# Hash attention with a SwiGLU block: four hash products side by side in batch one, the late hash block moved behind the sums

## The chip, the cores and the metric

The kernel runs on one core of one Trainium2 chip. The metric is the time of one execution on the device in microseconds (us); less is better. All runs of this study were correct and in the fast state. Single executions of one kernel differ by up to 5 us (the kernel before: 1007.44 to 1012.0 in 30 runs of one session), most by 1 to 3, so differences near 1 us are judged by ratios over many runs and by the traces together. Each run's record also has the mean clock that the chip granted to TensorE, 1.000 being full. Short names: PE is TensorE's matmul stream, PEld its weight loads, DVE is VectorE, ACT ScalarE, POOL GpSimd, SP the engine whose queue issues most transfers.

## The reference, cut to what matters

Four batches of eight heads, 768 positions, head size 64. A query may see a key only where both fall into the same hash bucket. The attention output goes through a SwiGLU block.

```python
q_bits = (np.einsum('bhsd,dk->bhsk', q, proj) > 0)      # proj: 64 x 6
k_bits = (np.einsum('bhsd,dk->bhsk', k, proj) > 0)
mask = q_bucket[:, :, :, None] == k_bucket[:, :, None, :]   # buckets: the bits as one number
scores = np.where(mask, scale * q @ k.T, -1e9)
attn = softmax(scores)                                  # sum + 1e-9 below
out = attn @ v
# then, on x = out with the heads side by side (3072 x 512):
y = (silu(x @ w_gate) * (x @ w_val)) @ w_out            # 512 -> 1536 -> 512
```

## The kernel before

Heads are handled in pairs, four pairs to a batch. Scores are formed transposed. The mask is a second product added to them: each side has a bf16 tile (`kb`, `qb`) of signs, six per head, and k's signs are multiplied by a large constant, so that one differing bit pushes the score far below. The tile has rows 0 to 31 for scores of head 0 and rows 64 to 95 for head 1; a per-row factor clears the bits of the other head.

```python
def score(u):                       # six units (c = 0..5) a half, two halves a pair
    for x, start in ((T, True), (bits, False)):       # scores, then the mask
        for h in range(2):
            nc.tensor.matmul(sc[h], x["k", n][rows, ks], x["q", n][rows, qs], ...)
    for h in range(2):
        nc.scalar.activation(weights(u)[:, h, 0:HQ], sc[h], AF.Exp, scale=SCALE)

def sign(name, half, to, ps):
    o = bits[name, n][to, half * HQ : (half + 1) * HQ]          # HQ = 384
    nc.scalar.activation(o, ps, AF.Sign, bias=nudge[to])
    if name == "k":
        return lambda: nc.vector.tensor_scalar(o, o, scalar1=times_k[to], ..., op0=ALU.mult)

def hash_bits(name, half):          # first batch: one product of full width (128 columns)
    ps = bank("hps")
    nc.tensor.matmul(ps[:, 0:HQ], hash_w, T[name, n][:, half * HQ : (half + 1) * HQ], ...)
    return [sign(name, half, slice(0, P), ps[:, 0:HQ])]

def hash_blocks():                  # later pairs: four products of 32 columns in one bank
    tile_ = bank("hps")
    for i, (name, half) in enumerate(...):
        nc.tensor.matmul(tile_[i * 32 : (i + 1) * 32, 0:HQ], hash_w[:, 0:32], T[name, n][...], ...)
    # ... then two signs for each of them (rows 0 and rows 64), eight in all,
    # and four multiplies on VectorE for k

def total(n):                       # softmax sums of a pair, and their reciprocals
    # four 32-column products, VectorE's reciprocal, then eight transfers on SyncE's queue
    # that spread the reciprocals to the rows of the attention output; later norm(n)
    ...
```

The order of work for half a pair, from the main loop:

```python
for c in range(NCH):
    score(u + c)
    if c == 1 and half == 0 and 0 < n <= NP: total(n - 1)      # batch one and its successor
    if c: add(u + c)                                           # VectorE sums the weights
...
for c in range(NCH): attend(u + c)
...
if half == 1 and n >= NP: total(n)
# from batch two on: some 56 projection passes of an earlier batch (in "atoms") come here, and
# the "chores" of the next pair stand among them:
chores = [None, steps.pop(0), None, steps.pop(0)] if half == 0 else [None, steps.pop(0)]
```

So in the second half of each later pair the hash block stands after the first eight projection passes. Up projections are shown as `up`, down projections as `po`.

The softmax here doesn't subtract the row's maximum and nothing guards it: scores larger than these inputs give would overflow.

## Time and profile before

| kernel before | |
|---|---|
| time, 3 first runs | 1008.49 us median (1008.31 to 1009.91) |
| profiled execution | span 1005.4 us, granted clock 1.000 |
| TensorE busy | 999.8 us (99%) |
| VectorE, ScalarE, GpSimd busy | 574.7, 417.4, 98.7 us |

The prediction below shows the chain and VectorE's timeline. One view must be added, because it became important later: the busy time by stretches of 20 us. Columns are the stretch, its length, then for PE, PEld, DVE, ACT and POOL the busy us and instructions, then the granted TensorE clock (1.00 is full), the DMA share and GB/s.

```profile
40.00:60.00 20.00, 20.00 (x125) 9.29 (x123) 16.33 (x24) 15.64 (x37) 4.27 (x8) 1.00 0.71 212
100.00:120.00 20.00, 19.63 (x109) 8.81 (x109) 17.06 (x22) 11.31 (x25) 3.25 (x6) 1.00 0.62 191
```

PE is busy in nearly every us of batch one, and its clock is at 1.00 in all of it. VectorE is busy for 16 to 17 of 20 us by the records, although it stands waiting only once a pair; the rest is the small gaps between its instructions. A busy share therefore does not say which of the two sets the pace.

### The profile page before, as it was taken

What the parts mean: (1) busy time and instruction counts of PE and PEld (TensorE: products, weight loads), DVE (VectorE), ACT (ScalarE), POOL (GpSimd) and SP (SyncE); (2) the same over time, 40 slices, a digit from 0 to 9 for tenths busy, and PEclk for the clock granted to TensorE, in tenths of its full rate; (3) what the DMA queues carried; (4) which work ended last, traced back from release to release, by engine and by line L of the source; (5) the groups of instructions that cost most, each with busy time, mean ns of one, the idle gap of its engine ahead of it and who ended that gap; (6) DMA issues with size and microseconds to landing.
All of it is one profiled execution on the core that took longest, in us unless ns stands there. A gap on an engine that the chain in (4) does not pass through costs nothing.

```text
span 1005.4 us, 12486 instructions
## 1 busy us (share of the span) xinstructions
PE 999.8 (99%) x4597; PEld 603.9 (60%) x4597; DVE 574.7 (57%) x919; ACT 417.4 (42%) x921; POOL 98.7 (10%) x192
## 2 busy tenths in 40 slices
PE   9999999999999999999999999999999999999998
PEld 4444455555576775555557776555555787555687
DVE  4788898887883624556464543545557342435421
ACT  7777457575424215335351323435444201222200
POOL 2222132231000000000000000000000000111000
PEclk9999999999999999999999999999999999999999
DMA  7777495886213032433331304242122011323101
GB/s 229 200 257 228 145 243 156 229 279 169 76 39 78 22 95 67 101 97 92 95 105 28 72 17 115 76 102 84 54 85 78 22 37 63 105 76 113 32 27 37
DMA packets 120029, 106.21 MB, mean 106 GB/s; under 512 B 89024, under 2 KB 103360, under 8 KB 119968
## 3 DMA queue, kind: packets, MB, share of 16 engines
q0 software_dynamic: 19104, 73.28, 22.8%
q1 hardware_dynamic: 100064, 31.94, 14.0%
q8 instruction: 36, 0.59, 0.3%
q10 hardware_dynamic: 800, 0.20, 0.1%
q14 instruction: 25, 0.20, 0.1%
HBM read 81.79 MB, written 17.30 MB: 99 GB/s over the span
## 4 chain that ended last, share of the span: by engine, by line
PE 89%; DVE 7%; SPq 2%; issue 1%; DMA 1%; DVEq 0%; ACT 0%
PE up L544 42%; PE po L544 21%; PE sc L455 12%; PE av L469 10%; SPq L513 2%; DVE acc L487 1%; PE sum L500 1%; DVE wo L508 1%; PE hps L402 1%; DMA wo<-wo 1%; DVE room L294 1%; PE hps L394 1%; DVE room L326 0%; DVE room L349 0%; DVE xT L520 0%
## 5 line engine op out<-in xcount | busy, mean ns | idle before, releaser
L544 PE MATMUL up<-xT,room 128*128 128x384 f32 x768 | 263.7, 490 | 0.4 <-DVE xT L520 0.4
L544 PEld LDWEIGHTS up<-xT,room 128*128 128x128 f32 x768 | 144.2, 190 | 110.3 <-issue 15.4
L544 PE MATMUL up<-xc,room 128*128 128x384 f32 x576 | 197.4, 487 | 0.0
L455 PE MATMUL sc<-qT,kT 64*128 64x384 f32 x768 | 160.3, 494 | 0.0
L544 PEld LDWEIGHTS up<-xc,room 128*128 128x128 f32 x576 | 109.7, 191 | 76.0 <-ACT hid L607 0.2
L548 DVE TENSOR_TENSOR c<-c,up 128x384 f32<-128x384 f32 x72 | 39.8, 553 | 179.7 <-PE up L544 178.5
L487 DVE TENSOR_TENSOR acc<-acc,A 128x768 f32<-128x768 f32 x128 | 122.7, 958 | 15.4 <-ACT A L458 2.6
L308 POOL DMA_DIRECT2D room<-ram x96 | 51.9, 541 | 717.9 <-PE up L544 710.3
L458 ACT ACTIVATE A<-sc 128x384 f32<-128x384 f32 x256 | 105.4, 505 | 4.9 <-PE sc L455 4.7
L679 ACT COPY o<-po 128x256 f32<-128x256 f32 x48 | 17.9, 372 | 196.5 <-PE po L544 196.5
L455 PEld LDWEIGHTS sc<-qT,kT 64*128 64x128 f32 x768 | 68.0, 187 | 50.7 <-issue 43.3
L469 PE MATMUL av<-A,vraw 128*64 128x384 f32 (+1 forms) x512 | 88.2, 487 | 0.0
L530 ACT ACTIVATE th<-c 128x384 f32<-128x384 f32 x72 | 37.6, 523 | 110.9 <-DVE c L531 83.4
L548 DVE TENSOR_TENSOR o<-o,po 128x256 f32<-128x256 f32 x36 | 15.1, 421 | 111.6 <-PE po L544 82.4
L458 ACT ACTIVATE room<-sc 128x384 f32<-128x384 f32 x128 | 54.4, 495 | 33.6 <-PE sc L455 33.6
L544 PE MATMUL po<-wo,hid 128*128 128x256 f32 x288 | 66.9, 382 | 0.0
L544 PE MATMUL po<-wo,room 128*128 128x256 f32 x288 | 66.6, 381 | 0.2 <-DVE room L548 0.2
L544 PE MATMUL po<-room,hid 128*128 128x256 f32 x288 | 66.1, 380 | 0.0
L607 ACT COPY c<-up 128x384 f32<-128x384 f32 x72 | 34.4, 478 | 74.5 <-PE up L544 74.3
L455 PE MATMUL sc<-qb,kb 64*128 64x384 bf16 x384 | 65.2, 323 | 0.0
L469 PEld LDWEIGHTS av<-A,vraw 128*64 128x64 f32 x512 | 36.8, 137 | 46.0 <-issue 45.4
L544 PEld LDWEIGHTS po<-wo,hid 128*128 128x128 f32 x288 | 54.2, 190 | 12.0 <-issue 4.9
(109 smaller groups left out, 998.3 us busy)
## 6 DMA issues: line engine op xcount, KB each, us to landing
room<-ram POOLq DMA_DIRECT2D x48, 512.0 KB, 4.7
room<-ram POOLq DMA_DIRECT2D x48, 384.0 KB, 3.9
vraw<-in_v_dram SPq DMA_DIRECT2D x16, 384.0 KB, 3.3
ram<-room POOLq DMA_DIRECT2D x12, 512.0 KB, 4.7
out_dram<-o SPq DMA_DIRECT2D x48, 128.0 KB, 1.7
room<-in_moe_w_out_dram POOLq DMA_DIRECT2D x10, 512.0 KB, 6.7
qraw<-in_q_dram SPq DMA_DIRECT2D x48, 96.0 KB, 3.1
hid<-in_moe_w_gate_dram POOLq DMA_DIRECT2D x9, 512.0 KB, 6.2
```

What stands on the lines that cost most here:

```text
L294: nc.vector.scalar_tensor_tensor(out=wi, in0=hi, scalar=-(1 << 31), in1=wi, op0=ALU.bitwise_and, op1=ALU.bitwise_or)
L308: nc.gpsimd.dma_start(places[k % 2][:, PARTS[go], :], ram[k % NG][:, PARTS[go], :])
L455: nc.tensor.matmul(sc[h], x["k", n][rows, ks], x["q", n][rows, qs], start=start, stop=not start)
L458: nc.scalar.activation(weights(u)[:, h, 0:HQ], sc[h], AF.Exp, scale=SCALE)
L469: nc.tensor.matmul(ps[h * D : (h + 1) * D, 0:width], raws["v", n][:, h, c, :], a[:, h, 0:width], start=c == 0, stop=c == NCH - 1)
L487: nc.vector.tensor_tensor(acc[n, half], acc[n, half], a[:, :, 0:HQ], op=ALU.add)
L513: nc.sync.dma_start(t[at : at + BLOCK, half, :], r[g : g + BLOCK, :])
L530: nc.scalar.activation(th, g, AF.Tanh, scale=0.5)
L544: nc.tensor.matmul(ps, a, x, start=start and i == 0, stop=i == len(pairs_) - 1, skip_group_check=True)
L548: nc.vector.tensor_tensor(o, a, b, op=op)
L607: nc.scalar.copy(tile_of(g, spot), c)
L679: nc.scalar.copy(o, c)
```

## The change

The intent was to take work off TensorE and ScalarE. All hash products become 32 columns wide and stand side by side, in batch one too. Only the low rows get their signs from ScalarE, one 32x384 sign per product. The high rows are made from the low ones ("spread"): k's by a VectorE multiply, q's by a VectorE copy in batch one and by a transfer later. Late hash blocks stand directly behind the sums; in batch one the block of the next pair stands behind the last score unit of a pair. The transposes of the first pair's second half move into its first two score units. The core of the diff, with cuts marked:

```diff
-    hash_w = konst.tile([P, P], FP32, tag="hash", name="hash")
+    hash_w = konst.tile([P, BLOCK], FP32, tag="hash", name="hash")
 ...
+    for t in (sides["k", 0], sides["q", 0], sides["q", 1]):
+        nc.gpsimd.memset(t, 0.0)
 ...
-        def hash_bits(name, half): ...
-        def hash_blocks(): ...          # two signs each, four multiplies
+        def hash_blocks(todo, own):
             tile_ = bank("hps")
+            for i, (name, half) in enumerate(todo):
+                nc.tensor.matmul(tile_[i * BLOCK : (i + 1) * BLOCK, 0:HQ], hash_w, ...)
+            low, high = slice(0, BLOCK), slice(D, D + BLOCK)
+            def sign(i, name, half):
+                nc.scalar.activation(bits[name, n][low, half * HQ : (half + 1) * HQ],
+                                     tile_[i * BLOCK : (i + 1) * BLOCK, 0:HQ], AF.Sign, bias=nudge)
+            def spread():
+                for name in sorted({name for name, _ in todo}):
+                    b = bits[name, n][:, ...]
+                    if name == "k":
+                        for to, times in ((high, times_k[1]), (low, times_k[0])):
+                            nc.vector.tensor_scalar(b[to], b[low], scalar1=times, ..., op0=ALU.mult)
+                    elif own:
+                        nc.vector.tensor_copy(b[high], b[low])
+                    else:
+                        nc.sync.dma_start(b[high], b[low])
 ...
         for x, start in ((T, True), (bits, False)):
+            if u < 2 and not start:
+                prepare_pair(1)
 ...
-            if u == 0 and c in (0, 1, 2, 4):
+            if u + c == 2 or not gating and half == 1 and c == NCH - 1:
                 prepare_pair(1)
 ...
+        chores = []
         if half == 1 and n >= NP:
             total(n)
+            if n + 1 < len(pairs):
+                chores = [None] + steps.pop(0)()      # the products right behind the sums
 ...
-            else:
-                chores = [None, steps.pop(0)]
```

More of the change, by code (lines that the diff above doesn't have):

```diff
@@ L142 @@
     rules = wraw.tile([P, PIECE, 2], I32, tag="words", name="rules").rearrange("p f w -> p (f w)")
-    rules = rules.bitcast(FP32)[:, 0 : 2 * P].rearrange("p (x r) -> p x r", r=P)
+    rules = rules.bitcast(FP32)[:, 0 : 3 * P].rearrange("p (x r) -> p x r", r=P)
     nc.gpsimd.memset(rules[:, 0, :], -(2.0**-120))
-    nc.gpsimd.memset(rules[:, 1, :], 0.0)
+    nc.gpsimd.memset(rules[:, 1:3, :], 0.0)
     groups = rules.rearrange("p x (g r) -> p x g r", r=HR)
@@ L149 @@
     for h in range(2):
-        g = groups[:, 1, h * D // HR + h, :]
+        g = groups[:, 1 + h, h, :]
         nc.gpsimd.memset(g[:, 0:NBITS], OFF / 2)
         nc.gpsimd.memset(g[:, NBITS : NBITS + 1], -NBITS * OFF / 2)
-    nc.vector.tensor_tensor(rules, rules, ident.unsqueeze(1).to_broadcast([P, 2, P]), op=ALU.mult)
-    columns = konst.tile([P, 2], FP32, tag="columns", name="columns")
+    nc.vector.tensor_tensor(rules, rules, ident.unsqueeze(1).to_broadcast([P, 3, P]), op=ALU.mult)
+    columns = konst.tile([P, 3], FP32, tag="columns", name="columns")
     nc.vector.tensor_reduce(out=columns, in_=rules, axis=AX.X, op=ALU.add)
-    nudge, times_k = (columns[:, x : x + 1] for x in range(2))
-    hash_w = konst.tile([P, P], FP32, tag="hash", name="hash")
+    nudge, *times_k = (columns[0:BLOCK, x : x + 1] for x in range(3))
+    hash_w = konst.tile([P, BLOCK], FP32, tag="hash", name="hash")
     nc.vector.memset(hash_w, 0.0)
@@ L162 @@
         nc.vector.tensor_copy(hash_w[rows, h * HR : h * HR + NBITS], two_proj[rows, :])
-    nc.vector.tensor_copy(hash_w[:, D : D + BLOCK], hash_w[:, 0:BLOCK])
     ones = konst.tile([P, BLOCK], FP32, tag="ones", name="ones")
@@ L383, in front @@
         bits["k", n] = sides["k", n % 2]
-        def sign(name, half, to, ps):
-            o = bits[name, n][to, half * HQ : (half + 1) * HQ]
-            nc.scalar.activation(o, ps, AF.Sign, bias=nudge[to])
-            if name == "k":
-                return lambda: nc.vector.tensor_scalar(o, o, scalar1=times_k[to], scalar2=None,
-                                                       op0=ALU.mult)
-        def hash_bits(name, half):
-            ps = bank("hps")
-            nc.tensor.matmul(ps[:, 0:HQ], hash_w, T[name, n][:, half * HQ : (half + 1) * HQ],
-                             start=True, stop=True)
-            return [sign(name, half, slice(0, P), ps[:, 0:HQ])]
@@ L398, in hash_blocks @@
-        def hash_blocks():
+        def hash_blocks(todo, own):
             tile_ = bank("hps")
-            for i, (name, half) in enumerate((name, half) for name in "kq" for half in range(2)):
-                nc.tensor.matmul(tile_[i * BLOCK : (i + 1) * BLOCK, 0:HQ],
-                                 hash_w[:, 0:BLOCK], T[name, n][:, half * HQ : (half + 1) * HQ],
+            for i, (name, half) in enumerate(todo):
+                nc.tensor.matmul(tile_[i * BLOCK : (i + 1) * BLOCK, 0:HQ], hash_w,
+                                 T[name, n][:, half * HQ : (half + 1) * HQ],
@@ L404, in hash_blocks @@
                                  start=True, stop=True)
-            def evict(name, half):
-                i = 2 * (name == "q") + half
-                ps = tile_[i * BLOCK : (i + 1) * BLOCK, 0:HQ]
-                for to in (0, D):
-                    scale = sign(name, half, slice(to, to + BLOCK), ps)
-                    if scale:
-                        more.append(scale)
-            more = []
-            return [lambda at=at: evict(*at) for at in
-                    (("k", 0), ("k", 1), ("q", 0), ("q", 1))] + [lambda: [f() for f in more] and None]
+            low, high = slice(0, BLOCK), slice(D, D + BLOCK)
@@ new lines, in sign @@
+            def sign(i, name, half):
[3 more added lines that the diff above has]
+                for name in sorted({name for name, _ in todo}):
+                    hs = [half for x, half in todo if x == name]
+                    b = bits[name, n][:, hs[0] * HQ : (hs[-1] + 1) * HQ]
+                    if name == "k":
+                        for to, times in ((high, times_k[1]), (low, times_k[0])):
+                            nc.vector.tensor_scalar(b[to], b[low], scalar1=times, scalar2=None,
+                                                    op0=ALU.mult)
+                    elif own:
+                        nc.vector.tensor_copy(b[high], b[low])
+                    else:
+                        nc.sync.dma_start(b[high], b[low])
@@ L418, in transpose_blocks, with hash_at_once @@
+            return [lambda i=i, at=at: sign(i, *at) for i, at in enumerate(todo)] + [spread]
+        def hash_at_once(todo):
+            *signs, spread = hash_blocks(todo, True)
+            for f in signs:
+                f()
+            return [spread]
         def transpose_blocks(name):
@@ L420, in transpose_blocks @@
             nc.vector.transpose(T[name, n], raws[name, n].rearrange("p c h d -> p (c h d)"))
+        order = [("q", 0), ("q", 1), ("k", 0), ("k", 1)]
         if n > NP:
-            return [lambda name=name: transpose_blocks(name) for name in "qk"] + [hash_blocks]
-        order = [("k", 0), ("k", 1), ("q", 0), ("q", 1)]
+            return ([lambda name=name: transpose_blocks(name) for name in "qk"]
+                    + [lambda: hash_blocks(order, False)])
         turns = [lambda x=x: transpose(*x) for x in order]
-        hashes = [lambda x=x: hash_bits(*x) for x in order]
         if n == 0:
-            return [turns[0], turns[2], hashes[0], hashes[2], turns[1], hashes[1], turns[3],
-                    hashes[3]]
-        return turns + hashes
+            return [turns[2], turns[0], lambda: hash_at_once([("k", 0)]),
+                    lambda: hash_at_once([("q", 0)]), turns[3], turns[1],
+                    lambda: hash_at_once([("k", 1), ("q", 1)])]
+        return turns[2:] + turns[:2] + [lambda: hash_at_once(order)]
     units = [(n, half, c) for n in range(len(pairs)) for half in range(2) for c in range(NCH)]
@@ L737 @@
             score(u + c)
-            if u == 0 and c in (0, 1, 2, 4):
+            if u + c == 2 or not gating and half == 1 and c == NCH - 1:
                 prepare_pair(1)
-                finish(rest)
+                if u == 0:
+                    finish(rest)
             if c == 1 and half == 0 and 0 < n <= NP:
@@ L748 @@
             steps = front(n + 1)
-        if not gating and u > 0:
+        if not gating and half == 0 and u > 0:
             prepare_pair(2)
@@ L758 @@
             load(n + 2)
-        if not gating:
+        if not gating and half == 0:
             prepare_pair(2 if u > 0 else 4)
@@ L768 @@
             continue
-        chores = []
-        if n + 1 < len(pairs):
-            if half == 0:
-                steps = front(n + 1)
-                chores = [None, steps.pop(0), None, steps.pop(0)]
-            else:
-                chores = [None, steps.pop(0)]
+        if n + 1 < len(pairs) and half == 0:
+            steps = front(n + 1)
+            chores = [None, steps.pop(0), None, steps.pop(0)]
         credit += 14 if n < 2 * NP else 15.75
```

## The prediction

> **What bounds the kernel now.** I read the page's busy line first, then the chain that ended last in order of time, then VectorE's timeline over the first 120 us, then the groups with shapes kept apart. The busy line, as engine, us, share and instructions:
>
> ```profile
> PE 999.8 (99%) x4597; PEld 603.9 (60%) x4597; DVE 574.7 (57%) x919; ACT 417.4 (42%) x921; POOL 98.7 (10%) x192
> ```
>
> By this line alone TensorE (PE) is the bound, and every us taken from it is a us of the run. The chain (start, length, what) says otherwise for the first batch:
>
> ```profile
> 35.51 0.83 PE sum L500 x8
> 36.36 2.57 DVE wo L508
> ...
> 116.12 2.02 DMA wo<-wo
> 118.46 1.03 DVE xT L520
> 119.53 15.10 PE up L544 x46
> 134.63 5.05 PE sc L455 x36
> 139.68 4.02 PE av L469 x24
> 143.70 0.78 PE sum L500 x8
> 144.48 2.78 PE up L544 x8
> 147.26 0.78 PE hps L402 x8
> 148.04 15.68 PE up L544 x48
> 163.72 5.04 PE sc L455 x36
> 168.77 4.04 PE av L469 x24
> 172.81 18.26 PE up L544 x56
> ```
>
> From 36.36 to 119.53 all of the chain is VectorE (DVE), the eight queue issues behind each reciprocal, and their landing; from 119.53 on it is nearly all PE. VectorE's timeline confirms the first part. One round of a head pair:
>
> ```profile
> 77.67 4.15 DVE L487 TENSOR_TENSOR acc<-acc,A 128x768 f32<-128x768 f32 x4
> 81.73 0.54 DVE L389 TENSOR_SCALAR kb<-kb,columns 128x384 bf16<-128x384 bf16 x2
> 82.19 0.42 DVE L292 TENSOR_SCALAR room<-room 128x512 int32<-128x512 int32 x1
> ...
> 86.11 2.55 DVE L508 RECIPROCAL wo<-sum 128x384 f32<-128x384 f32 x1
> 88.58 0.90 DVE L483 SCALAR_TENSOR_TENSOR acc<-room 128x768 f32<-128x768 f32 x1
> 89.58 4.15 DVE L487 TENSOR_TENSOR acc<-acc,A 128x768 f32<-128x768 f32 x4
> 95.46 1.02 DVE L520 SCALAR_TENSOR_TENSOR xT<-xT,e,wo 128x768 f32<-128x768 f32 x1 [1.74 <-DMA wo<-wo]
> ```
>
> Only the last row waits, and for transfers that VectorE's own reciprocal started. From 46.71 to 118.46 VectorE waits three times (1.81, 1.74, 2.03), always there, and never for PE or ScalarE. So PE and VectorE both run at about 24 us a pair (reciprocals at 61.69, 86.11, 108.81), and VectorE is the one that waits for nobody. Shortening PE there buys nothing.
>
> **What the Trainium skill says.** "TensorEngine Tiling (Array Packing)", Key Properties: tiles work independently, but "Changing tiling mode (not just tile) drains the TensorE". The trace agrees with both: a block of four 32-column products (eight passes, passes of 498 ns each) takes 0.78 us, and each block that cuts into the 128-column stream costs extra (worked out below). "VectorE: DVE Perf Modes", the perf-mode tier table: a bf16 scalar multiply or copy in SBUF reaches 4 results a cycle at 0.96 GHz, so doubling 384 columns to 768 should add about 0.10 us. The trace has only 384 columns, at 308 to 315 ns; the slope is untested. "Perfetto Trace Analysis", Optimization Strategy: a kernel can have several regimes with different contended engines; here 36 to 119 us is one and the rest another. "DMA: Bandwidth & Descriptors", Anatomy of one DMA (its figure is for the GpSimd path): about 2 us fixed; the trace, for the SyncE queue, shows 1.91 to 2.54 us from the last issue to the landing of the spread reciprocals.
>
> **The change, part by part.**
>
> ```profile
> L394 PE MATMUL hps<-kT,hash 128*128 128x384 f32 x20 | 8.1, 518 | 0.2 <-ACT kT L380 0.2
> L394 PE MATMUL hps<-qT,hash 128*128 128x384 f32 x20 | 8.0, 512 | 0.0
> L402 PE MATMUL hps<-kT,hash 128*32 128x384 f32 x44 | 9.2, 498 | 0.0
> L389 DVE TENSOR_SCALAR kb<-kb,columns 32x384 bf16<-32x384 bf16 x44 | 13.6, 308 | 1.1
> ```
>
> (Groups: shapes, count, busy us, mean ns, idle before.)
>
> 1. PE, batch one. Pairs 1 to 4 pay two blocks of two full-width hash products now, 1.49 + 1.49 us in the chain (26.65, 32.16); one block of four side by side costs 0.78. That is 2.2 us x 4 pairs = 8.8 us of PE work, plus about 1 us at pair 0. It lies beside VectorE's chain, so I count none of it after 36 us.
>
> 2. VectorE, batch one. Two multiplies of 384 columns take VectorE 0.46 us (81.73 to 82.19). In their place stand, per pair, a multiply to the high rows, a multiply of the low rows that waits for it, and a copy of q, all 32x768. Estimate from the trace's 308 ns plus the skill's 0.10: 0.41 + 0.03 (wait) + 0.33 + 0.27 (the last two overlap the one before by 0.09, as the 0.54 us for two of 0.315 shows) = 1.04, so +0.6 us; if the columns go at half that rate, +0.9. I take +0.65. Pairs 1 to 4 all fall on the chain that ends at 118.46: +2.6 us.
>
> 3. The start. PE waits for the first signs were filled with work; the moved transposes do the same. One hash product less in front of the first attention is 0.8 us, but the last one is now behind the third score unit, with two exponentials, its sign and two multiplies before the fourth unit's mask can run. Following the durations (sign 0.57, multiply 0.31, exponential about 0.4), that mask is ready near 13.6 us and PE gets there near 12.8. So PE gains about 0.4 at 16 us. VectorE also waited 1.18 us for the sums before the first reciprocal (36.36); the sums now come over 2 us earlier, so that goes. Together -1.6 us.
>
> Batch one: -1.6 + 2.6 = **+1.0 us** at the point where PE's chain resumes (119.53 becomes about 120.5).
>
> 4. Later batches, PE. Eleven times a hash block cuts into a stream of projections. With it: 0.78 + 2.78 + 0.78 + 15.68 = 20.02 us from the sums to the next scores. A stream not cut takes 18.26 (172.81). Behind the sums, which use the same four 32-column tiles, the block should need only its two passes, 2 x 0.325 = 0.65. So 0.78 + 0.65 + 18.26 = 19.69, -0.33 us each. The cut down-projection (0.78 + 2.79 + 0.78 + 15.74 = 20.09, against 18.33 uncut) gives the same. 11 x 0.33 = **-3.6 us**, all on the chain, as PE has no slack there.
>
> 5. ScalarE and VectorE later: four signs instead of eight (0.57 each), two multiplies instead of four. Neither is the bound there: worth nothing, except that around 268 to 291 us VectorE is in the chain for a moment; -0.2 us at most.
>
> 6. The transfer of q's signs: eleven of 48 KB on the queue that has just issued eight for the reciprocal (147.48 to 152.53, at worst 204.18 to 210.99). One more issue and a 2 to 3 us landing make about 214; the scores start near 220. Hidden. The banks do not add a wait: in the built program the first projection that must wait for the reciprocal still stands fourteen products behind the sums.
>
> Sum: 1008.5 + 1.0 - 3.6 - 0.2 = 1005.7; I say **1006.0 us**.
>
> **The rivals.** (a) PE is the bound throughout, as its 99% suggests: all 9.8 us of part 1 and the 3.6 of part 4 come out, about 995 us. Against it: VectorE's timeline with no wait for PE. (b) VectorE becomes worse than I think: the three spread instructions run at one result a cycle (0.95 us each), +2.4 us a pair, or PE's late masks push back the reciprocals too. Then batch one loses 8 us, and the run is near 1013. Against it: 308 ns for 384 columns, which one result a cycle (400 ns) could not reach. (c) The hash block behind the sums still pays its drain or its weight load: part 4 is then half, -1.8, and the run 1008. (d) The transfer of q's signs comes late, or holds up loads behind it on its queue: a wait at each first mask, up to 1 us x 11, near 1016. The 6 us of slack speak against it.
>
> **Range and chances.** Batch one may be anything from -1 (spread cheaper, start better) to +3; part 4 from -1.5 to -4. That spans 1003.3 to 1009.8; the middle of it, with some weight on a partial (a), gives 1003.0 to 1009.0 for 8 in 10. Two per cent is 20 us, which no rival reaches: faster 0.01, same 0.98, slower 0.01.
>
> **What would show it.** In the changed profile PE should be idle 2 to 4 us per pair in batch one, waiting for VectorE's spread signs before the first mask of pairs 2, 3 and 4 and for the reciprocal before the attention; PE's busy time should fall by over 10 us while the span falls by 2 or 3. The chain should still be VectorE's up to about 120.5. The spread should take about 1.0 us a pair on VectorE. Sums and hash should stand as one piece of about 1.43 us followed by projections of 18.26. I am wrong if PE stays gapless before 120 us, if up projections resume near 110, or if a first mask of a later pair waits for the transfer.

## The result, and the profile after

| | before | after, first timing | after, timed again |
|---|---|---|---|
| median of fast runs, us | 1009.04 (4 runs) | 1008.07 (4 runs, 1007.60 to 1008.85) | 1007.58 (13 runs); before in that session 1008.50 |
| ratio to before, 95% interval | | 0.9991 (0.9974 to 1.0008) | 0.9992 (0.9984 to 1.0000) |
| span of the profiled execution, us | 1005.4 | 1005.8 | 1004.3 |
| TensorE, VectorE, ScalarE busy, us | 999.8, 574.7, 417.4 | 991.4, 577.2, 392.3 | 989.7, 576.7, 392.2 |

A ratio here is the one on record for the fast runs of both kernels; it is close to the ratio of their means, but not quite that of the medians. The verdict is "the same": a saving of about 0.9 us, where 2.5 were predicted. The number on record, 1006.0 us, lies 2 us below the first median and the median lies inside the range.

TensorE's work did fall; the busy line of the changed kernel:

```profile
PE 991.4 (99%) x4597; PEld 600.8 (60%) x4597; DVE 577.2 (57%) x904; ACT 392.3 (39%) x877; POOL 101.0 (10%) x195
```

That is 8.4 us less of PE (10.1 in the second profile, where less of it ran at a lowered clock) and 25.1 us less of ScalarE, for about 0.9 us of time. The chain of the changed kernel from the end of batch one on (start, length, what):

```profile
109.68 1.44 PE sum L506 x8
...
119.53 18.26 PE up L550 x56
137.78 5.05 PE sc L461 x36
142.83 4.02 PE av L475 x24
146.85 0.78 PE sum L506 x8
147.63 0.65 PE hps L391 x8
148.28 18.26 PE up L550 x56
...
803.27 36.46 PE po L550 x168
```

From 146.85 to 166.54 the late part reads exactly as worked out: 0.78 + 0.65 + 18.26 = 19.69 us, where 20.02 stood. But the first projections of batch one's end are done at 137.78, where before it was 134.63: batch one is 3.15 us longer, not 1.0. The same program in its second profile:

```profile
120.10 1.03 DVE xT L526
121.17 15.10 PE up L550 x46
136.28 5.05 PE sc L461 x36
```

Here it is 1.65 us longer, and VectorE and its transfers lead up to 121.17, as the prediction said, while in the first profile PE itself is on the chain from 108.26 on. So the same kernel takes two different ways through batch one. VectorE's spread of pair 2, first profile:

```profile
56.04 0.85 DVE L406 TENSOR_SCALAR kb<-kb,columns 32x768 bf16<-32x768 bf16 x2
56.93 0.35 DVE L409 COPY qb<-qb 32x768 bf16<-32x768 bf16 x1
```

The next instruction starts at 57.31, so the spread takes 1.27 us from the first multiply to it, where the two old multiplies left room for the next after 0.46 us (81.73 to 82.19). With a gap of 0.12 more between the last addition of weights and the first multiply, I read +0.93 us a pair. PE's view of the same place, first profile:

```profile
57.04 0.61 PE L461 MATMUL sc<-qb,kb 64*128 64x384 bf16 x2 [2.64 <-DVE kb L406]
58.39 1.51 PE L506 MATMUL sum<-acc,ones 128*32 128x384 f32 x8
83.11 0.61 PE L461 MATMUL sc<-qb,kb 64*128 64x384 bf16 x2 [2.49 <-DVE kb L406]
108.26 0.61 PE L461 MATMUL sc<-qb,kb 64*128 64x384 bf16 x2 [2.75 <-DVE kb L406]
109.61 1.51 PE L506 MATMUL sum<-acc,ones 128*32 128x384 f32 x8
```

PE waits for the signs of pairs 2, 3 and 4 before the first mask, as predicted. What was not predicted is that the sums behind two of these waits take 1.51 us instead of 0.85. The stretches around the fourth pair's wait show why (columns as above):

```profile
105.50:108.20 2.70, 0.01 (x2) 0.00 (x0) 2.50 (x5) 0.00 (x0) 0.00 (x0) 1.00 0.96 269
110.00:112.00 2.00, 2.00 (x12) 0.66 (x6) 1.80 (x3) 0.60 (x2) 0.54 (x1) 0.50 0.26 38
112.00:114.00 2.00, 2.00 (x14) 1.06 (x11) 2.00 (x2) 0.95 (x3) 0.00 (x0) 0.75 0.65 242
```

After these 2.7 us without work the granted clock falls to half. Adding up the stretches from 108.2 to 114 (0.88 of 1.8 us, 0.50 of 2, 0.75 of 2), 1.7 us of PE's time is lost. In the second profile the same sums at the fourth pair run at full speed:

```profile
59.04 1.50 PE L506 MATMUL sum<-acc,ones 128*32 128x384 f32 x8
109.25 0.85 PE L506 MATMUL sum<-acc,ones 128*32 128x384 f32 x8
```

The wait in front of them was the same 2.75 us. So the length of the wait alone does not decide: 2.64 us drew it and 2.49 did not in the first profile; 3.17 drew it, 1.53 and 2.75 did not in the second. Over the six kept profiles with these waits left in (the two here, old_place, spread_twice, scale_later and short_memset; three waits each), all seven waits of 2.83 us or more were followed by a lowered clock, five of the seven between 2.36 and 2.75, and none of the four up to 2.11. The Trainium skill, "TensorE: Matmul & The Clock Gate", Part 1: The HAM clock gate, describes this: the clock is halved after an idle window of about 3.4 us, and the window runs free, not aligned to the kernel. This case's trace agrees with the half (0.50), and equal waits with different outcomes fit a free-running window, though no run here tests that; that waits of 2.6 to 2.8 us can be enough is not what I would have read from it.

How often this happens can be read from the record, since every run has its mean granted clock. One drop of 1.7 us is 0.0017 of the run, so the first profile, with two of them, shows 0.997. The kernel before is at 1.000 in nearly all of its runs. Of the 13 runs of the change timed again, nine are at 0.995 to 0.997 and take 1007.19 us on average, and four are at 0.993, twice the loss, and take 1008.72. The deep loss so costs about 1.5 us, in about a third of the runs. The records do not say at which pair it fell.

The late part shows one wait that has grown. A line of ScalarE's timeline:

```profile
222.23 0.67 ACT L279 ACTIVATE wo<-words 128x512 f32<-128x512 f32 x1 [1.77 <-DMA words<-in_moe_w_out_dram]
```

This scaling of an output weight stands in ScalarE's order ahead of the gates and exponentials of the scores at 222.56. Its load was issued at 214.42, behind another transfer in GpSimd's order, and landed 7.79 us later. Before, the same load was issued just as long before the scores (8.14 us) but landed after 6.7; ScalarE waited 1.46 us for it and was done earlier. Why the load now takes longer to land (7.2 to 8.2 us in the kept profiles with the late part, 7.0 with the hash block at its old place) was not isolated. PE is held up: the six score units take 6.42 us (222.56 to 228.98), where they took 5.40 before (220.08 to 225.48) and take 5.04 when nothing holds them.

### The profile page after: what moved, and what is told of

Its sections match the earlier page's. It is cut to its first block, busy times and chain, and to the rows that moved or that the text cites. A ratio compares the mean times of both kernels' runs of the same rounds, so it can differ in the third digit from the quotient of the medians.

```text
span 1005.8 us, 12454 instructions
## 1 busy us (share of the span) xinstructions
PE 991.4 (99%) x4597; PEld 600.8 (60%) x4597; DVE 577.2 (57%) x904; ACT 392.3 (39%) x877; POOL 101.0 (10%) x195
## 4 chain that ended last, share of the span: by engine, by line
PE 89%; DVE 6%; DMA 1%; SPq 1%; issue 1%; ACT 1%; DVEq 0%; POOL 0%
PE up L550 43%; PE po L550 21%; PE sc L461 12%; PE av L475 10%; DVE acc L493 1%; SPq L519 1%; PE sum L506 1%; PE hps L391 1%; DMA words<-in_moe_w_out_dram 1%; DVE wo L514 1%; DVE room L295 1%; DVE room L327 1%; DMA wo<-wo 1%; DVE room L293 0%; PE idle L134 0%
## 5 line engine op out<-in xcount | busy, mean ns | idle before, releaser
L550 PE MATMUL up<-xT,room 128*128 128x384 f32 x768 | 260.9, 488 | 0.0
L461 PE MATMUL sc<-qb,kb 64*128 64x384 bf16 x384 | 66.2, 325 | 8.4 <-DVE kb L406 8.4
```

What stands on the lines that cost most here:

```text
L550: nc.tensor.matmul(ps, a, x, start=start and i == 0, stop=i == len(pairs_) - 1, skip_group_check=True)
```

## The experiments

To compare profiles I use two points that all have: E, the end of the first block of up projections (134.63 before), and P, the start of the 168 down passes near 803. E tells what batch one costs, P minus E what the eleven late blocks cost. Before, P - E is 803.14 - 134.63 = 668.51; with eleven savings of 0.33 it should be 664.88. A third number, R, is the time from the first to the fourth reciprocal on VectorE: three rounds of its chain. R holds VectorE's waits too, for transfers and sometimes for PE's sums; W is R without those that its timeline lists, so VectorE's own work and small gaps. The profile is that of one run, in late_pool and scale_later of the slowest one.

| kernel | ratio to before (95%), runs | E | P - E | R | W |
|---|---|---|---|---|---|
| before | 1 | 134.63 | 668.51 | 72.45 | 66.17 |
| after, first profile | 0.9991 (0.9974 to 1.0008), 4 | 137.78 | 665.49 | 75.00 | 68.94 |
| after, second profile | 0.9992 (0.9984 to 1.0000), 13 | 136.28 | 665.46 | 75.20 | 68.83 |
| late part alone | 0.9964 (0.9951 to 0.9978), 5 | 135.33 | 665.95 | 72.92 | 66.19 |
| hash block at its old place | 1.0023 (1.0015 to 1.0031), 14 | 137.77 | 668.44 | 75.95 | 68.94 |
| hash early, all pairs | 1.0004 (0.9996 to 1.0012), 13 | 139.66 | 666.45 | 75.89 | 68.98 |
| hash early, not pair 1 | 0.9984 (0.9978 to 0.9991), 21 | 136.62 | 666.39 | 74.96 | 68.85 |
| spread twice | 1.0033 (1.0020 to 1.0046), 8 | 142.42 | 666.51 | 79.65 | 72.49 |
| filler products | 0.9983 (0.9977 to 0.9990), 21 | 138.13 | 665.02 | 75.38 | 68.96 |
| q by transfer in batch one | 1.0215 (1.0198 to 1.0233), 4 | | | | |
| late part, multiplies on GpSimd | 0.9985 (0.9978 to 0.9992), 19 | 140.17 | 665.63 | 77.57 | 66.51 |
| scaling later | 0.9981 (0.9974 to 0.9987), 21 | 138.97 | 665.66 | 76.46 | 68.92 |
| late part, scaling later | 0.9962 (0.9950 to 0.9974), 5 | 135.25 | 665.11 | 72.79 | 66.17 |
| short memsets | 0.9990 (0.9983 to 0.9996), 22 | 136.40 | 665.46 | 75.01 | 68.85 |

W falls into clear groups: 66.2 in the three kernels with the old batch one on VectorE, 68.8 to 69.0 wherever the spread is in it. E is coarser: the late part alone, whose batch one is the kernel before's, still has it 0.7 us later, because transfers landed later and the start was slower.

My theory after the result: the late part gives its 3.6 us; batch one loses about 2 us because VectorE's chain carries a spread of +0.93 us a pair; PE's lowered clock adds up to 1 us more on top. Rivals: the late part did not give what its chain shows; or batch one is set by PE's waits and their clock, not by VectorE.

### late_only: the late part without batch one's part

The kernel before, with only the late half of the change.

```diff
-            return [lambda ...: transpose_blocks(name) for name in "qk"] + [hash_blocks]
+            return ([lambda ...: transpose_blocks(name) for name in "qk"]
+                    + [lambda: hash_blocks([("q", 0), ("q", 1), ("k", 0), ("k", 1)])])   # as changed
...
+        chores = []
         if half == 1 and n >= NP:
             total(n)
+            if n + 1 < len(pairs):
+                chores = [None] + steps.pop(0)()
```

> The kernel before with only the later batches changed (hash block behind the sums, four signs, q's signs spread by a transfer); batch one as before. My theory: each of eleven halves loses 0.33 us of TensorE, nothing else changes, so -3.6 us against the kernel before, span near 1002, and the sums stand 0.78 us, the hash block 0.65 us, projections 18.26 us. Rival (the late part brings nothing, or its transfer makes the masks wait): within 1 us of before. Rival (the late load of the output weights near 215 us, 1.0 us of idle TensorE in the changed kernel, belongs to the late part): -2.6 us.

Measured: 1005.63 us (1004.82 to 1006.41), ratio 0.9964, so -3.2 us against the shared runs of the kernel before (1008.81) and about -3.6 by the ratio. The late part gives a gain of the size worked out, and it beats the full change by some 2 to 3 us. P - E is 665.95, not 664.88: about 1 us goes back in the wait for the output weight, which this kernel has too. So the trace shows -2.6 us up to P, and the ratio's interval runs from -2.2 to -4.9; that its middle is just 3.6 says less than it seems.

### old_place: the change with the hash block among the projections again

```diff
-                chores = [None] + steps.pop(0)()
+                chores = [None, steps.pop(0)]
```

> The changed kernel with the hash block put back among the projections (still four signs and the transfer). My theory: +3.6 us against the changed kernel, so 2.5 to 4 us slower than the kernel before, because batch one alone costs about 3 us. Rival (the place of the block is worth nothing and the gain lies elsewhere): as the changed kernel.

Measured: 1011.40 us, ratio 1.0023, some 3.1 us slower than the changed kernel by the ratios. P - E is 668.44, the kernel before's 668.51 again, and E is unchanged at 137.77. So place alone decides over the 3 us: four signs rather than eight, and the transfer for q, are worth nothing there.

### spread_twice: more of VectorE's cost

Three more multiplies of 32x768 a pair on VectorE in pairs 1 to 4, into a tile that nothing reads.

```diff
             def spread():
+                if own and n > 0:
+                    for name, x in (("k", 1), ("k", 0), ("q", 0)):
+                        nc.vector.tensor_scalar(spare, bits[name, n][low], scalar1=times_k[x], ...)
```

> The changed kernel with three more 32x768 bf16 multiplies on VectorE per pair in batch one (pairs 1 to 4), into a spare tile, ahead of the spread. My theory (VectorE's chain sets batch one): about 1.3 us more per pair, +4.5 to +5.5 us in all. Rival (TensorE sets it, VectorE has slack): less than 1 us.

Measured: 1012.04 us, ratio 1.0033: +4.1 us against the changed kernel. W rises from 68.9 to 72.49, so 1.2 us a pair, three multiplies of 0.41; R rises more, to 79.65, as VectorE also waits 0.85 us there for PE's sums. Four pairs of 1.2 us are 4.8 us of work, for 4.1 us of time: batch one's length follows VectorE's work nearly one for one. W gives the spread's own cost too: 68.83 to 68.98 against 66.17 to 66.19 is 0.88 to 0.94 us a pair, whatever PE's clock did. The clock is not without effect on VectorE, though: its fourth reciprocal waits for PE's sums for 0.17 us in the first profile of the change, 0.83 in old_place and 1.12 in scale_later, each time behind a drop. One rival this run leaves: the added multiplies also delay PE's masks. early_later below takes these waits away.

### warm: filler products in the waits

Ten bf16 products of zeros, which nothing reads, in front of the first mask of pairs 2 to 4.

```diff
+            if not start and c == 0 and half == 0 and 2 <= n <= NP:
+                fill = bank("fill")
+                for _ in range(10):
+                    nc.tensor.matmul(fill, filler[:, 0:P], filler, start=True, stop=True)
```

> The changed kernel with ten bf16 products of zeros (128x512) on TensorE in the waits before the first masks of pairs 2, 3 and 4; nothing reads them. My theory: TensorE's granted clock falls (0.91 to 0.96 in these stretches) because it sat idle[...]; with the filler it stays at 1.00, the sums behind pair 4's mask take 0.78 us instead of 1.44, and the run gains about 1.0 us against the changed kernel, no more, as VectorE's chain stays. Rival (the slow stretch has nothing to do with the idle time): clock and time unchanged or worse.

Measured: 1007.28 us, ratio 0.9983, about 0.9 us below the changed kernel; the two intervals overlap (0.9977 to 0.9990 against 0.9984 to 1.0000). The granted clock is 1.000 in all 21 runs and 1.00 in every stretch of batch one, and the sums at 58.67, 84.77 and 109.95 all take 0.85 us. So it is the idle wait that lowers the clock. Its runs take 1007.23 us on average, as the changed kernel's nine at 0.995 to 0.997 do (1007.19): what the filler saves is the deep loss. In its profile E is nevertheless 138.13, because the last spread of reciprocals landed 1.5 us later than in the other profiles (VectorE waited 3.07 us for it, against 1.56). With PE quick again, VectorE's chain is what PE waits for (1.33 us at 123.03).

### early_hash and early_later: the hash before the second half's scores

Give VectorE its spread earlier, so that PE need not wait. `early_hash` does it for all four pairs, `early_later` leaves pair 1 as in the change.

```diff
+        if not gating and half == 1:              # early_later: ... and n > 0
+            prepare_pair(1)
+            finish(rest)
         for c in range(NCH):
             score(u + c)
-            if u + c == 2 or not gating and half == 1 and c == NCH - 1:
+            if u + c == 2:                        # early_later: or n == 0 and half == 1 and c == NCH - 1
```

> The changed kernel with batch one's hash block and its spread moved ahead of the second half's scores, so that VectorE spreads the signs before that half's five sums instead of behind them. VectorE's work is the same. My theory: TensorE's waits of 2.5 to 2.75 us before the first masks of pairs 2, 3 and 4 go, and with them the slow stretches of TensorE behind them (granted clock 0.91 to 0.96 there); the first batch then ends when VectorE's chain ends, about 1.9 us earlier than in the changed kernel. Rival (VectorE's total alone sets the end): unchanged within 0.5 us.

Measured: 1009.33 us, ratio 1.0004: no gain, the expectation failed, although the clock is at 0.999 to 1.000 in all 13 runs. For pair 1 VectorE now stands for the signs, which ScalarE gives only after a row of exponentials:

```profile
26.54 0.85 DVE L406 TENSOR_SCALAR kb<-kb,columns 32x768 bf16<-32x768 bf16 x2 [4.04 <-ACT kb L397]
```

That delays everything behind it on VectorE, and the first reciprocal comes at 37.88, where it was 36.19.

> As early_hash, but pair 1 is left as in the changed kernel: early_hash lost 3.1 us at once there, because VectorE stood 4.04 us waiting for the first signs, and my expectation for it failed for that. My theory: the waits before the masks of pairs 2 to 4 go without that price, and with them the slow clock; -1 to -2 us against the changed kernel. Rival (VectorE's total alone): unchanged within 0.5 us.

Measured: 1007.40 us, ratio 0.9984, about 0.8 us below the changed kernel, less than the 1 to 2 us expected and more than the rival's 0.5, with intervals that overlap. The mask waits and the lowered clock are gone, but PE now waits elsewhere in each pair: 1.34 us in front of the hash products for q's transpose, and 0.50 to 1.67 us in front of the attention for the reciprocal. W is 68.85, as before the edit, and E is 136.62, where the change has 136.28 and 137.78. PE's waits moved; VectorE's chain did not.

### q_transfer: q's signs by transfer in batch one too

```diff
-            *signs, spread = hash_blocks(todo, True)
+            *signs, spread = hash_blocks(todo, n == 0)
```

> The changed kernel with q's signs spread by a transfer in batch one too (pairs 1 to 4), so that VectorE has one 32x768 copy less a pair. My theory (VectorE's chain): 0.38 us x 4 = -1.5 us against the changed kernel, if the transfer lands before the two multiplies are done; the masks come at the same distance behind the multiplies. Rival (the transfer of 2 to 3 us takes the place of the copy as the wait): unchanged or slower by up to 1 us a pair.

Measured: 1030.42 us, ratio 1.0215. It was to take 0.3 us a pair off VectorE, and cost 22 us. The rival named a late transfer, at a much smaller size. The queue's view around pair 2, and PE's at its mask:

```profile
57.03 0.37 SPq L81 DMA_DIRECT2D vraw<-in_v_dram  x1
57.50 0.80 SPq L411 DMA_DIRECT2D qb<-qb  x1
```

```profile
67.19 0.48 PE L461 MATMUL sc<-qb,kb 64*128 64x384 bf16 x1 [8.37 <-DMA qb<-qb]
```

ScalarE has q's signs ready at 54.3. The transfer stands in the queue's order behind the load of a later v and is issued at 57.50, 3.2 us later. Then it takes 9.6 us to land, where the median of its kind is 1.9: from 57 to 67 us the DMA engines are busy at a share of 0.95 to 1.04 with v's 384 KB and with weights. In later pairs the same transfer meets no such crowd, and no mask waits for it.

### late_pool: batch one's multiplies on GpSimd

The late part alone, with k's sign multiplies of pairs 1 to 4 on GpSimd, to relieve VectorE instead of loading it.

```diff
-                return lambda: nc.vector.tensor_scalar(o, o, ...)
+                return lambda: (nc.gpsimd if n else nc.vector).tensor_scalar(o, o, ...)
```

> The kernel that had only the later batches changed, with batch one's two multiplies of k's signs (128x384, pairs 1 to 4) on GpSimd instead of VectorE. My theory: VectorE's chain loses 0.46 us x 4 = 1.8 us; TensorE has little slack there, so -1.0 to -1.8 us against that kernel, span near 1001 to 1002. Rival (TensorE sets batch one in that kernel): unchanged. Rival (GpSimd is slow at it, or slows VectorE): slower.

Measured: 1007.09 us, ratio 0.9985: 2.1 us slower than the late part alone.

```profile
84.56 2.64 POOL L389 TENSOR_SCALAR kb<-kb,columns 128x384 bf16<-128x384 bf16 x2
```

One multiply takes 1.25 to 1.85 us there, against 0.31 on VectorE, and it stands in order behind weight loads that GpSimd issues. PE waits 2.82 us for it once, the clock falls (0.83 from 80 to 100 us), and the sums then come late for VectorE (1.34 and 2.21 us). VectorE slows down beside it as well: two of its instructions take 1.10 and 0.95 us there that take 0.69 in the late part alone, and W is 66.51, no shorter than 66.19 although six multiplies of 0.31 us are gone. This profile is of the slowest of the 19 runs. In 16 of them the clock is at 1.000, and these still take 1006.84 us on average, against 1005.57 for the late part alone, so the lowered clock is not the main loss.

### scale_later and late_scale: the output weight's scaling behind the exponentials

One pair of ScalarE instructions is moved, in the changed kernel and in the late part alone.

```diff
-            if 6 < part < 11 or u == LATE and part > 10:
+            if (6 < part < 11 or u == LATE and part > 10) and progress["scaled"] != 30:
                 scale_ahead()
```

> The changed kernel with one pair of scaling instructions on ScalarE (the output-weight piece whose load is issued at 214.42 us) moved from in front of the exponentials of the scores behind them; nothing else moves. If ScalarE's 1.77-us wait for that load at 222.23 us is what gave back about 1 us of the gain of the later batches: the wait is gone from ScalarE's stream, the scores at 222 to 226 us run without the stall, and the time is about 1.0 us below the changed kernel (some 1007.1 against 1008.1). Rival: the stall is hidden, or the same us is lost again a little later, because VectorE or GpSimd then stands for that piece: within 0.3 us of the changed kernel.

Measured: 1006.73 us (1005.23 to 1008.97), ratio 0.9981, so about 1.1 us below the changed kernel by the ratios, with intervals that overlap. Its profile does not bear the whole gain out: ScalarE's wait at this place is gone, the six score units run in 5.04 us without a stop, and the attention at 228.79 comes 5.04 us after the scores' start, against 6.42 in the changed kernel. But at the next scores the same thing happens with a later weight:

```profile
254.41 0.59 PE L461 MATMUL sc<-qT,kT 64*128 64x384 f32 x1 [0.79 <-DVE c L537]
```

P - E is 665.66, no better than 665.49. This profile is of the slowest of the kernel's 21 runs, and at the deep loss of clock (0.993), so it does not stand for them. The runs at equal clocks do: 15 at 0.995 to 0.998 take 1006.44 us on average against 1007.19 in the changed kernel, six at 0.993 take 1007.98 against 1008.72. That is 0.75 and 0.74 us of gain, the size that late_scale shows below.

> Late part alone on the kernel before, with the same scaling moved. Expected: about 1.0 us below the late part alone (1005.63), so 1004.6, the best of all versions, with the stall gone at the same place. Rival: no change, 1005.6.

Measured: 1004.95 us (1004.67 to 1005.26), ratio 0.9962, against 1005.63 and 0.9964 for the late part alone. Here the wait at the next scores is only 0.24 us, and P - E falls from 665.95 to 665.11. The trace shows 0.8 us of gain, the medians 0.7, and the ratios cannot tell the two kernels apart. It has the lowest median of all versions and beats both kernels of this case.

### short_memset: the three added memsets half as long

```diff
-        nc.gpsimd.memset(t, 0.0)
+        nc.gpsimd.memset(t.bitcast(FP32), 0.0)
```

> The changed kernel with its three added memsets on GpSimd written as 32-bit words, half as many elements. If these memsets, which share the time of VectorE's copies of the projection columns at the start, cost the start something, the first scores come up to 0.7 us earlier (8.25 us now) and the time falls by up to 0.7 us. Rival: the start is set by the loads and PE's clock phase, and the time stays within 0.3 us of the changed kernel's 1008.1.

Measured: 1007.46 us, ratio 0.9990: as the changed kernel (0.9992), the rival was right. The memsets take 0.42 + 0.77 us instead of 0.74 + 1.41, and the first scores come at 7.76 instead of 8.25 us; yet in the second profile of the unedited change they come at 7.46. How long the nine warm-up products take (3.57 to 4.02 us in two profiles of one kernel) outweighs the memsets.

### after_again: the change timed again

> The changed kernel itself, unedited, timed in as many rounds as the experiments. Its first timing (ratio 0.9991, interval 0.9974 to 1.0008) is too wide to set against variants that differ by 1 us. If warm, early_later and scale_later each save about 1 us against it, its ratio to the kernel before comes out at 0.9988 to 0.9995 (a saving of 0.5 to 1.2 us). Rival: the changed kernel itself is at 0.9983 or below, and these three variants save nothing.

Measured: 1007.58 us (1006.07 to 1009.09), ratio 0.9992. The saving of about 0.8 to 0.9 us stands, and so do the three variants' gains as best estimates, though each interval overlaps this one. Its profile gave the comparison shown above: the same program, with E 1.5 us earlier.

## Why the prediction was right or wrong

- **What bounds the kernel: right.** Batch one follows VectorE (spread_twice: three more multiplies, +4.1 us), the rest follows PE (old_place, late_only). Of PE's 8.4 us less work, the late part has 2.7 (997.1 us of PE are busy in late_only), and these were paid back; the other 5.7, in batch one, brought nothing in themselves. Rival (a) falls.
- **Part 1, PE's work in batch one: right** that none of it counts. Taking it away had a side effect that the prediction saw only in half: it named the idle waits of 2 to 4 us, but counted them as free. They are not, because the clock can fall after them: 1.7 us of PE's time at the fourth pair in the first profile, of which 0.9 reached the end of batch one (E is +3.15 where VectorE's last normalization, 118.46 before and 120.72 after, is +2.26). In the second profile no drop fell there, and E is +1.65 with the normalization at 120.10, +1.64.
- **Part 2, the spread: the term that was mis-sized.** "I take +0.65" a pair measured +0.93, or +0.88 to +0.94 by W. The slope was right: the Trainium skill's "VectorE: DVE Perf Modes", the perf-mode tier table, put 0.10 us on 384 more columns, and the trace shows 0.31 against 0.41 us for the multiply and 0.25 against 0.35 for the copy, 0.10 more in each. The small gap came on top: 1.27 us from the first multiply to the next instruction, against 1.04 in the sum, and 0.12 more in front. Four pairs make +3.7 instead of +2.6. Rival (b) does not come in its size (2.4 us a pair), but its second half, late masks that push back the reciprocals, does in small: 0.17 to 1.12 us at the fourth pair, behind a drop of the clock.
- **Part 3, the start: about right, but it varies.** The spread of pair 1 stands in front of the first reciprocal, so parts 2 and 3 together predicted -1.6 + 0.65 = -0.95 there. It moved from 36.36 to 36.19 and to 35.37, so -0.17 and -0.99; the 1.18-us wait did go. Less the spread's 0.93, the start gave -1.1 and -1.9. Parts 2 and 3 together gave +1.64 to +2.26 at VectorE's last normalization, in place of +1.0; part 2's error alone is 1.1 us.
- **Part 4, the late blocks: right to the digit for one block.** 0.78 + 0.65 + 18.26 us stands in the trace; rival (c), half the gain, falls with old_place (+3.1 us, give or take about 1.1 with both intervals) and with P - E.
- **Part 5: right** that fewer signs and multiplies are worth nothing; the 0.2 us were not seen. Instead a wait grew that no part had named: for the load of an output weight, 0.6 us net in both profiles of the change (665.5 against 664.9), about 1 us in the late part alone.
- **Part 6, the transfer: right** for later pairs: no mask waits for it, so rival (d) falls. q_transfer shows that this depends on the queue: the same transfer in batch one waited up to 8.4 us.
- **The sum.** In the profiles: +1.65 to +3.15 for batch one, -3.6 for the late blocks, +0.6 for the new wait, so -1.4 to +0.2; measured -0.9. The predicted -2.5 misses by 1.6 us, and the range held because it let batch one go to +3, not because the chance of a lowered clock was seen. The sign on PE's busy time, "over 10 us" less, came out at 8.4 in the first profile and 10.1 in the second. What stays open: at which pair the drop falls over many runs, since a run's record has only its mean clock; and why the output weight's load lands later with the late part.

## What to carry to other kernels

Before trading work from the busiest engine to another, find the engine that waits for nobody in that stage: here 5.7 us off a 99% busy TensorE bought nothing in batch one, and 0.9 us a pair put on a 57% busy VectorE was paid in full. Look at the granted clock of every run, not of the profiled one alone: it splits runs that look like mere scatter. Small blocks that use another tile shape belong next to others of that shape: moving one block by eight passes gave 0.33 us each time, the whole gain of the change. Take a change with several parts apart: here the late part alone (-3.6 us by its ratio) is worth four times the whole.

## What the Trainium skill lacked or had wrong

- "TensorE: Matmul & The Clock Gate", Part 1: it speaks of an idle window of about 3.4 us. Here waits of 2.64, 2.75 and 3.17 us were followed by a granted clock of 0.50 (and one of 2.36 in spread_twice by 0.50 to 0.60), while a second 2.75 and waits of 2.49 and 1.53 us were not; one drop cost 1.7 us of PE's time. Keeping ten zero products in the wait held the clock at 1.00.
- "TensorEngine Tiling (Array Packing)", Key Properties: it says that a mode change drains the engine, but gives no size. Here one block of four 32-column products costs 0.33 us more among 128-column products than behind others of its shape.
- "GPSIMD Engine Reference", Engine selection: it calls GpSimd about line-rate for operations with one input. Here a 128x384 bf16 multiply by a per-row scalar, an operation with one tensor input, took 1.25 to 1.85 us on it and 0.31 on VectorE.
- "DMA: Bandwidth & Descriptors", Anatomy of one DMA: its figure, about 2 us fixed, is for transfers that GpSimd issues; the median of 48-KB transfers on SyncE's queue is near it here (1.9 us). It gives no figure for a transfer that meets busy engines: one of 48 KB, issued behind a 384-KB load while the DMA share stood near 1.0, took 9.6 us.
